# Delta-rule attention and an MLP on one core: another order of ScalarE's and VectorE's work in the opening

## The chip, the core and the metric

The kernel runs on one core of a Trainium2 chip. The core has TensorE (matmul), VectorE, ScalarE, GpSimd, and SyncE, which issues most of the DMAs; the five run at the same time, each takes its own instructions in the order in which they were written, and semaphores hold an instruction until what it needs is there. The metric is the device time of one execution in microseconds (us); lower is better. Times given as medians come from several executions; a profile is of one execution.

## The reference

```python
def _attn_ref(q, k, v, beta):                 # (4, 8, 768, 48): batch, heads, steps, width
    k_n = k / (np.linalg.norm(k, axis=-1, keepdims=True) + 1e-06)
    state = np.zeros((B, H, D, D))
    for t in range(S):
        kt, vt, bt = (k_n[:, :, t], v[:, :, t], beta[:, :, t, None])
        y[:, :, t] = np.einsum('bhd,bhde->bhe', q[:, :, t], state)
        v_old = np.einsum('bhde,bhd->bhe', state, kt)
        state = state + bt[:, :, :, None] * np.einsum('bhd,bhe->bhde', kt, vt - v_old)
    return y

def _moe_ref(x, w_in, w_out):                 # x: y as (3072, 384); d_ff 2048
    h = x @ w_in
    g = h * np.clip(h + 3.0, 0.0, 6.0) / 6.0
    return g @ w_out
```

The output of a recurrent attention (a state matrix for each batch and head, updated by the delta rule) is the input of an MLP with a hard swish.

## The kernel before

**Tiling.** The 768 steps are cut into 24 chunks of 32. A tile has the 4 batches' 32 steps on its 128 partitions. Inside a chunk the recurrence is a triangular system, whose inverse X turns the values less the old state's answer (R) into the new values (Z); between chunks the state is carried on. The MLP takes blocks of two chunks (256 tokens).

**For a chunk t.** `prep` (word p in the list below) scales the keys by their norm (GpSimd, L510), turns keys and queries on TensorE (`pt`, L524), copies them on ScalarE (`KQ`, L532), makes the scores on TensorE (`sc`, L547) and takes them out on VectorE with a mask (`L` and `LB`, L558). `chain` (h) reads the state (`ks`, L806), makes R (L901, L909), applies X (`pz`, L827), copies the result to Z on ScalarE (tile `R`, L927), and updates the state (`su` L938, `state` L956). Its output part (y) makes y (`py` L827; for chunk 0 a copy on ScalarE, L861), turns it (`yt`, L873) and copies it to `xT` on ScalarE (L877), the MLP's input.

**The inverses.** Chunk 0 has its own (`product`). Chunks 1 to 4 are one group: `halves_of` (word i1) waits for the scores of all four, transposes them (L469), eliminates the halves of all problems step by step on VectorE (L730, L735; 28 small instructions in a chain) and transposes back (L473). `join` (x1, x2, ...) then makes one chunk's inverse whole: a transpose (L694), a product on TensorE (`pi`, L684), L698 and L702 on VectorE, a second `pi`, and a copy to `X` on ScalarE (L710). `pz` of that chunk waits for this copy.

**The weights.** `w_in` and `w_out` arrive in a wide format in 16 pieces, 0 to 15 (word w issues a load) and are converted. ScalarE does four steps for a piece (word a, `scales`, L356), VectorE three (word c, `convert`: L378, L383, L389). The last of VectorE's steps needs all four of ScalarE's; and ScalarE's first step of piece i writes the buffer that VectorE's last step of piece i - 2 reads.

**The MLP in the opening.** The first half block (token half a) is made as soon as chunk 0's `xT` is there: word ua issues the products for 128 columns of `w_in` (`ph`, L994; "two more chunks" in the change are two such words), ra their relu on ScalarE (L1001), and ga the "rest", a minimum and product on VectorE (L1004), after which the PSUM buffer is free. There are four such buffers, shared with `pt`, `pi`, `pz`, `py`, `yt`.

**What sets the order.** Everything up to chunk 5 and the first three down and up passes is written in the order of a list of words, `ORDER`: each word runs one step of one of these generators, and `x*3` is three steps. A step's instructions go to the end of their engines' queues. So the list alone decides what stands ahead of what on each engine; an assertion (`needs`) refuses a list in which a step's inputs have not been issued. After the list a plan in the loop over chunks takes over; it is the same in both kernels.

Of the kernel before, what the change touches and what calls it, by code (L numbers as in the profile page):

```python
# [22 lines left out]
k*2 B*3 k*2 n0 k*2 z B s*2 n0*6 k*2 q*2 n1 q n1 q w k p0 z*3 k n1*2 k*2 n1*2 z p0*2 s k p0*3 a k a  # L23
m0 a n2 m1 p0 x0*2 w q x0 n1 x0*3 c*2 n2 a k s p1*2 a s*2 k q s*2 x0 n2 k*2 c x0 n2 x0 w q a*4 q p1
n2 k*2 a x0 m2 p1 c*2 p1 n2*3 b1 q b0 s p1 x0 q w x0 n2 q*2 c*3 x0 n4 k p1 k p2*2 x0*2 a*2 c a*2 q*3
a*2 w v p3*2 q x0 q n4 p2*2 c p2 v c n4*2 a*3 z v n4 c a m3 v c p2 n4*2 q p2 k c b2 h0 c h0 w a*2 h0
p4*2 a*2 m4 p3 q*4 h0 q k w p4*2 c*5 v*2 p3 k p3*3 k*2 p4*2 v*2 p4 m6 k a w a w i1*3 k i1*7 a i1*2 a
i1*2 v i1*2 k b3 k y0 c y0*3 ua*2 ra*2 i1*3 w v ga v a*3 i1*2 ua i1 h1 i1 q w ua ra ua i1 ra*2 ga i1
k ua a*2 ra ga i1 ga ua ra ua ra i1 ga i1*4 ua ga n5 x1*2 k x1 c a ra v a*2 ga x2 k*2 ga*2 ua*2 x1
ra*2 x1*2 ua h1*2 n5 k ga c ra ga*2 h1 c y1*2 ua ra w ga ua ra x2 n5 ga y1*2 ua ra ga h1 v*3 n5*2 k  # L30
y1*2 ua a ra x2 ub*2 a n5 rb*2 h1 x3 ga c*2 v W a h2 y2 gb ub rb gb x2 gb ub*2 n5*2 b4 rb n5 x2*2 h2
gb rb gb m5 a n5*2 y2 ub rb gb v c q*2 v q*5 n5 ub n5 rb gb h2 c h2 q ub y2 h2 y2 rb ub p5 b5 rb
gb*2 a*2 x3 p5 ub y2*2 k p5*2 h2 rb h3 p5 gb h3 ub*2 q rb gb rb gb ub a x3 p6 v c x4 x3 rb gb ub p7
rb gb y3 c*2 v c p7*2 y3 v p7*2 b6 x3 q x3 ub p6 h3 a p6 c p5*2 rb gb k m7 w p6 h3 u p6 k*2 q*3 a*2
y3 a p6 c y3 v y3*2 u n9 v k q a c a c*2 u*2 ru gu w k a*2 c a*2 x4 c*2 ru p7 a gu k u a*2 p7 p6 m8
u*3 a k u*2 k h3 w ru*2 a*2 gu*2 x4 c*2 x4 k c*2 a p8 k a*2 u ru k h3 u*2 h4 ru a b8 gu k gu y4 p8*3
u h4 k*2 c q k*9 q u p8*2 x4 k ru k*2 gu k c n9 q u q*2 p8 k*2 b7 n9*2 i2 u x4 q i2*2 q ub ru gu u
rb gb i2*2 h4*2 u*2 i2 ru i2*6 y4 i2 gu i2*7 u i2 ru gu i2 u*3 ru i2*4 gu ru i2*2 v i2 c gu u*3 a u
ru c i2 u*2 i2 gu i2*3 q i2*5 y4 h4 n9 i2 e*2 n9*2 i2*4 q i2 y4 e n9 u ru i2*3 u i2 ru*2 gu h4 u n9
i2*2 u i2 e i2*6 y4 u k n9*3 u gu i2 y4 n9 i2 p9 q i2*2 gu  # L40
"""


# [1521 lines left out]
```

## Time and profile before

| | us |
|---|---|
| median of 3 runs | 663.66 |
| lowest, highest | 663.46, 663.9 |
| the profiled execution | 662.06 |
| its span in the profile | 660.3 |
| TensorE busy in the span | 632.5 (96%) |
| VectorE busy | 499.2 (76%) |
| ScalarE busy | 282.3 (43%) |
| GpSimd busy | 225.1 (34%) |

The shares are averages over the whole span. The page's second part cuts the span into 40 slices of 16.5 us and gives each engine's busy tenths in each; the changed words act in slices 3 to 5. The granted TensorE clock of the whole execution is 0.997 of full speed. In ten-microsecond windows of the opening, TensorE is busy 6.33 us (30 to 40), 6.16 (40 to 50), 9.42 (50 to 60) and 9.06 (60 to 70); VectorE 8.82, 9.25, 9.28 and 9.41; ScalarE 7.71, 9.38, 7.08 and 7.21. TensorE's matmuls are pipelined and their ends are modelled, so a full TensorE is not TensorE at its peak.

### The profile page before, as it was taken

The numbers are of one execution on the slowest core, as the hardware profiler recorded it, in microseconds if no ns is written. First come the engines' busy times: TensorE is split into PE (matmuls) and PEld (weight loads), VectorE is DVE, ScalarE is ACT, GpSimd is POOL, SyncE is SP. The second block draws the span as 40 slices with busy tenths as digits, with TensorE's granted clock in tenths as the row PEclk, the third lists the DMA queues.
The fourth block names the chain that finished last, engine by engine and source line by source line (L and its number), as shares of the span: only waits on it lengthen the run. The fifth ranks groups of instructions, "written<-read, shape, count | busy, mean of one in ns | idle before, by whom it ended". The sixth has DMA issues, their size and how long they took to land.

```text
span 660.3 us, 26640 instructions
## 1 busy us (share of the span) xinstructions
PE 632.5 (96%) x11640; PEld 569.2 (86%) x11640; DVE 499.2 (76%) x1170; ACT 282.3 (43%) x548; POOL 225.1 (34%) x352
## 2 busy tenths in 40 slices
PE   2768999999999999999999999999999999999997
PEld 2658987776689989999999999999999999999997
DVE  5899877798657988758988848979658998456354
ACT  5887689332243154154154244244244144153250
POOL 6531022003661353553254354164051242331430
PEclk9998999999999999999999999999999999999999
DMA  7888346202040030041030030020020020000000
GB/s 174 204 198 235 77 102 164 51 25 43 9 87 18 3 74 3 3 90 22 3 74 3 2 74 3 2 63 2 3 50 2 3 49 3 23 18 2 26 1 24
DMA packets 88692, 33.28 MB, mean 50 GB/s; under 512 B 80224, under 2 KB 83424, under 8 KB 88576
## 3 DMA queue, kind: packets, MB, share of 16 engines
q1 hardware_dynamic: 88224, 31.29, 20.8%
q8 instruction: 91, 1.49, 0.9%
q10 hardware_dynamic: 352, 0.30, 0.2%
q14 instruction: 25, 0.20, 0.1%
HBM read 26.84 MB, written 4.72 MB: 48 GB/s over the span
## 4 chain that ended last, share of the span: by engine, by line
PE 91%; DVE 3%; DMA 2%; SPq 1%; ACT 1%; issue 1%; DVEq 0%
PE po L1226 28%; PE ph L1066 27%; PE ph L994 9%; PE po L1162 6%; PE ks L806 4%; PE su L938 3%; PE pt L524 3%; PE pz L827 3%; PE py L827 3%; PE sc L547 2%; PE yt L873 1%; DMA spare<-in_moe_w_in_dram 1%; PE pi L684 1%; DMA w_out<-in_moe_w_in_dram 1%; SPq L168 1%
## 5 line engine op out<-in xcount | busy, mean ns | idle before, releaser
L1066 PE MATMUL ph<-xT,w_in 128*128 128x128 f32 (+1 forms) x720 | 156.8, 321 | 0.0
L1030 POOL TENSOR_TENSOR g<-g 128x256 f32<-128x256 f32 (+1 forms) x144 | 88.6, 616 | 104.7 <-ACT g L1080 99.1
L1066 PEld LDWEIGHTS ph<-xT,w_in 128*128 128x128 f32 x720 | 116.8, 191 | 6.7
L1226 PE MATMUL po<-w_out,g 128*128 128x192 f32 x640 | 110.6, 326 | 0.0
L1226 PEld LDWEIGHTS po<-w_out,g 128*128 128x128 f32 x640 | 104.6, 190 | 0.5
L1080 ACT ACTIVATE g<-ph 128x512 f32<-128x512 f32 x72 | 43.1, 598 | 105.1 <-PE ph L1066 105.1
L1226 PE MATMUL po<-spare,g 128*128 128x192 f32 x480 | 86.7, 332 | 0.0
L1226 PEld LDWEIGHTS po<-spare,g 128*128 128x128 f32 x480 | 77.2, 190 | 1.8
L994 PE MATMUL ph<-xT,w_in 128*128 128x128 f32 (+1 forms) x384 | 72.0, 338 | 0.6 <-ACT xT L877 0.6
L1236 POOL TENSOR_TENSOR o<-o,u 128x192 f32<-128x192 f32 x18 | 13.3, 739 | 163.8 <-ACT o L1233 86.6
L994 PEld LDWEIGHTS ph<-xT,w_in 128*128 128x128 f32 x384 | 59.6, 195 | 7.7 <-ACT xT L877 0.8
L1093 DVE TENSOR_TENSOR g<-ph,g 128x256 f32<-128x256 f32 x72 | 30.2, 419 | 46.8 <-PE ph L1066 33.5
L759 DVE TENSOR_TENSOR pr<-A 128x30 f32<-128x30 f32 (+9 forms) x150 | 57.3, 382 | 3.3
L1212 DVE TENSOR_TENSOR g<-g 128x512 f32<-128x512 f32 x80 | 56.1, 722 | 3.5 <-PE po L1226 3.5
L1113 DVE SCALAR_TENSOR_TENSOR g<-o,g 128x512 f32<-128x512 f32 x72 | 52.6, 730 | 7.8 <-ACT o L1110 7.7
L764 DVE TENSOR_TENSOR A<-A,pr 128x30 f32<-128x30 f32 (+9 forms) x150 | 55.1, 367 | 3.3
L1110 ACT ACTIVATE o<-g,halves 128x512 f32<-128x512 f32 x72 | 52.2, 725 | 11.3 <-DVE g L1113 8.4
L1066 PE MATMUL ph<-beta_tok,sums_in 128*128 128x128 f32 x288 | 55.9, 275 | 0.0
L356 ACT ACTIVATE spare<-spare,places 128x768 uint16<-128x768 uint16 (+1 forms) x56 | 52.8, 947 | 3.2 <-DMA kf<-in_k_dram 1.6
L1233 ACT ACTIVATE o<-po 128x192 f32<-128x192 f32 x40 | 13.3, 332 | 82.7 <-PE po L1226 79.2
L510 POOL TENSOR_TENSOR kb<-kf,inv 128x384 f32<-128x384 f32 x24 | 21.7, 907 | 75.5 <-issue 43.1
L1162 PE MATMUL po<-w_out,g 128*128 128x384 f32 x128 | 45.4, 490 | 0.0
(141 smaller groups left out, 1019.1 us busy)
## 6 DMA issues: line engine op xcount, KB each, us to landing
kf<-in_k_dram SPq DMA_DIRECT2D x96, 48.0 KB, 2.6
qb<-in_q_dram SPq DMA_DIRECT2D x96, 48.0 KB, 2.4
vf<-in_v_dram SPq DMA_DIRECT2D x96, 48.0 KB, 2.1
out_dram<-o SPq DMA_DIRECT2D x90, 48.0 KB, 1.6
spare<-in_moe_w_in_dram SPq DMA_DIRECT2D x4, 768.0 KB, 6.6
w_out<-in_moe_w_in_dram SPq DMA_DIRECT2D x4, 768.0 KB, 6.1
w_out<-in_moe_w_out_dram SPq DMA_DIRECT2D x4, 768.0 KB, 5.8
spare<-in_moe_w_out_dram SPq DMA_DIRECT2D x4, 768.0 KB, 5.2
```

The costliest lines, as they stand in the source:

```text
L356: nc.scalar.activation(out=z, in_=z if n else d.bitcast(I16)[:, :, :, 3], func=func, bias=places[:, n : n + 1], scale=scale,)
L759: nc.vector.tensor_tensor(out=pv, in0=A[:, j + 1 :, j].unsqueeze(2).to_broadcast([n, w, j]), in1=A[:, j, 0:j].unsqueeze(1).to_broadcast([n ...
L764: nc.vector.tensor_tensor(out=A[:, j + 1 :, 0:j], in0=A[:, j + 1 :, 0:j], in1=pv, op=ALU.subtract)
L994: nc.tensor.matmul(ph[:, cols], lhsT=w_in[:, s, f * 128 : (f + 1) * 128], rhs=xT[:, s, cols], start=(s == 0), stop=(s == NKT - 1),)
L1030: nc.gpsimd.tensor_tensor(out=out, in0=a, in1=b, op=op)
L1066: nc.tensor.matmul(ph[:, n], lhsT=w, rhs=x, start=start, stop=stop, skip_group_check=True)
L1080: nc.scalar.activation(out=gt, in_=ph[:], func=ACTF.Copy)
L1110: nc.scalar.activation(out=r, in_=g, func=ACTF.Relu, bias=half, scale=1.0 / 6.0)
L1113: nc.vector.scalar_tensor_tensor(out=g, in0=r, scalar=1.0, in1=g, op0=ALU.min, op1=ALU.mult)
L1162: nc.tensor.matmul(pos[c][:], lhsT=gs[blk, f // 2][:, f % 2, c * P : (c + 1) * P], rhs=w_out[:, f, :], start=(f == 0), stop=(f == NFC - 1),)
L1212: nc.vector.tensor_tensor(out=A(f, *out, 4), in0=A(f, *a, 4), in1=A(f, *b, 4), op=op)
L1226: nc.tensor.matmul(ps[n][:], lhsT=A(f - f % 2, *a)[:, f % 2], rhs=b[:, f], start=(f == 0), stop=(f == HF - 1),)
```

## The change

Only the list of words differs; it has 782 words in both kernels, and each word occurs as often. ScalarE's copies of Z of chunk 0 (called R in the kernel's tiles), of the turned keys and queries of chunks 3 and 4, and of y of chunk 0 are issued ahead of conversion steps that stood before them. VectorE's steps of the conversion stand at other places: three of them (L389 of one piece, L378 and L383 of the next) stood ahead of the scores of chunks 3 and 4 and are issued later. Two more words ua (two column groups of the first half block) stand ahead of the first product of the join of chunk 1, and the words ra, ga and c around it move with them. TensorE turns the queries of chunk 3 ahead of `su`. GpSimd's and SyncE's orders stay as they were.

As instructions, from the fourth scale step of piece 3 on: ScalarE before had the four scale steps of piece 4, R, four of piece 5, keys 3, keys 4, queries 3, queries 4, four of piece 6, y, xT. ScalarE now has two of piece 4, R, keys 3, one, queries 3, one, one of piece 5, keys 4, queries 4, two, y, one, four of piece 6, xT. Further on, piece 8's four scale steps stood between the relus and stand now together behind relu 10, ahead of relu 11 and the first copy to X.

The diff (of the list's lines that differ, up to the last word that does):

```diff
-a*2 w v p3*2 q x0 q n4 p2*2 c p2 v c n4*2 a*3 z v n4 c a m3 v c p2 n4*2 q p2 k c b2 h0 c h0 w a*2 h0
-p4*2 a*2 m4 p3 q*4 h0 q k w p4*2 c*5 v*2 p3 k p3*3 k*2 p4*2 v*2 p4 m6 k a w a w i1*3 k i1*7 a i1*2 a
-i1*2 v i1*2 k b3 k y0 c y0*3 ua*2 ra*2 i1*3 w v ga v a*3 i1*2 ua i1 h1 i1 q w ua ra ua i1 ra*2 ga i1
-k ua a*2 ra ga i1 ga ua ra ua ra i1 ga i1*4 ua ga n5 x1*2 k x1 c a ra v a*2 ga x2 k*2 ga*2 ua*2 x1
-ra*2 x1*2 ua h1*2 n5 k ga c ra ga*2 h1 c y1*2 ua ra w ga ua ra x2 n5 ga y1*2 ua ra ga h1 v*3 n5*2 k
+a*2 w v p3*2 q x0 q n4 p2*2 c p2 v c n4*2 a*2 z v n4 c m3 v c p2 n4*2 q p2 k c b2 h0*2 p3 a w p3*2
+h0 a h0 p4*2 p3 a m4 q*4 c p3 q k w p4*2 c p4*2 c v*2 p4 k*3 v*2 a m6 k y0 a y0 a*2 w a w i1*3 k
+i1*7 a i1*2 a i1*2 c v i1*2 k b3 k y0*2 ua*2 ra*2 i1*3 w v ga v a*3 i1*2 ua i1 h1 i1 q w ua ra ua i1
+ra*2 ga i1 k ua a ra ga i1 ga ua ra ua ra i1 ga i1 ua i1*2 ra ga ua ra ga i1 n5 x1*2 ga c*2 k ua x1
+c a c a v a*2 x2 k*2 ga x1 ra x1*2 ua h1*2 n5 k ga c ra ga*2 h1 c y1*2 ua ra w ga ua ra x2 n5 ga
...
```

More of the change, by code (lines that the diff above doesn't have):

```diff
@@ L30 @@
-ra*2 x1*2 ua h1*2 n5 k ga c ra ga*2 h1 c y1*2 ua ra w ga ua ra x2 n5 ga y1*2 ua ra ga h1 v*3 n5*2 k
[L31 to L39, printed above, removed]
@@ L40 @@
-i2*2 u i2 e i2*6 y4 u k n9*3 u gu i2 y4 n9 i2 p9 q i2*2 gu
+a*2 w v p3*2 q x0 q n4 p2*2 c p2 v c n4*2 a*2 z v n4 c m3 v c p2 n4*2 q p2 k c b2 h0*2 p3 a w p3*2
[3 more added lines that the diff above has]
+c a c a v a*2 x2 k*2 ga x1 ra x1*2 ua h1*2 n5 k ga c ra ga*2 h1 c y1*2 ua ra w ga ua ra x2 n5 ga
@@ new lines @@
+y1*2 ua ra ga h1 v*3 n5*2 k y1*2 ua a ra x2 ub*2 a n5 rb*2 h1 x3 ga c*2 v W a h2 y2 gb ub rb gb x2
+gb ub*2 n5*2 b4 rb n5 x2*2 h2 gb rb gb m5 a n5*2 y2 ub rb gb v c q*2 v q*5 n5 ub n5 rb gb h2 c h2 q
+ub y2 h2 y2 rb ub p5 b5 rb gb*2 a*2 x3 p5 ub y2*2 k p5*2 h2 rb h3 p5 gb h3 ub*2 q rb gb rb gb ub a
+x3 p6 v c x4 x3 rb gb ub p7 rb gb y3 c*2 v c p7*2 y3 v p7*2 b6 x3 q x3 ub p6 h3 a p6 c p5*2 rb gb k
+m7 w p6 h3 u p6 k*2 q*3 a*2 y3 a p6 c y3 v y3*2 u n9 v k q a c a c*2 u*2 ru gu w k a*2 c a*2 x4 c*2
@@ L41 @@
+ru p7 a gu k u a*2 p7 p6 m8 u*3 a k u*2 k h3 w ru*2 a*2 gu*2 x4 c*2 x4 k c*2 a p8 k a*2 u ru k h3
+u*2 h4 ru a b8 gu k gu y4 p8*3 u h4 k*2 c q k*9 q u p8*2 x4 k ru k*2 gu k c n9 q u q*2 p8 k*2 b7
+n9*2 i2 u x4 q i2*2 q ub ru gu u rb gb i2*2 h4*2 u*2 i2 ru i2*6 y4 i2 gu i2*7 u i2 ru gu i2 u*3 ru
+i2*4 gu ru i2*2 v i2 c gu u*3 a u ru c i2 u*2 i2 gu i2*3 q i2*5 y4 h4 n9 i2 e*2 n9*2 i2*4 q i2 y4 e
+n9 u ru i2*3 u i2 ru*2 gu h4 u n9 i2*2 u i2 e i2*6 y4 u k n9*3 u gu i2 y4 n9 i2 p9 q i2*2 gu
 """
```

## The prediction

> **What bounds the kernel now.** I read the page first: slices, then the chain that ended last.
>
> ```profile
> span 660.3 us, 26640 instructions
> PE   2768999999999999999999999999999999999997
> ## 4 chain that ended last, share of the span: by engine, by line
> PE 91%; DVE 3%; DMA 2%; SPq 1%; ACT 1%; issue 1%; DVEq 0%
> ```
>
> TensorE is full from the fourth slice on, and the list of its waits has none between 62 and 655 us. So a delay of TensorE at about 65 us reaches the end whole, and only the opening, before about 61 us, has idle time to save. The changed words act from 36 to 70 us. Next the timeline of that stretch, TensorE first:
>
> ```profile
> 36.03 1.50 PE L827 MATMUL pz<-vf,X 32*32 32x48 f32 x64
> 39.29 1.27 PE L938 MATMUL su<-R,sums_in 32*64 32x48 f32 x61 [1.75 <-ACT R L927]
> 41.31 0.44 PE L938 MATMUL su<-R,sums_in 32*64 32x48 f32 x3 [0.75 <-issue]
> 49.92 0.55 PE L873 MATMUL yt<-ident,y 128*128 128x128 f32 x3 [2.41 <-ACT y L861]
> 61.24 0.72 PE L684 MATMUL pi<-X,sums_in 16*32 16x16 f32 x64 [0.94 <-DVE sums_in L694]
> 63.43 0.73 PE L684 MATMUL pi<-X,sums_in 32*32 32x16 f32 x64
> 64.95 0.95 PE L827 MATMUL pz<-R,X 32*32 32x48 f32 x64
> ```
>
> Columns are start, duration, engine, line and tile, and in brackets the wait. See the two waits for ScalarE (R, y), a hold of 0.75 us in the middle of `su` that no engine ended ("issue"), and the wait of the first join product `pi` for VectorE. ScalarE and VectorE in the same stretch:
>
> ```profile
> 38.77 0.47 ACT L927 ACTIVATE R<-pz 128x384 f32<-128x384 f32 x1
> 45.51 3.98 ACT L356 ACTIVATE spare<-spare,places 128x768 uint16<-128x768 int16 x4
> 50.51 0.49 ACT L877 ACTIVATE xT<-yt 128x384 f32<-128x384 f32 x1 [0.64 <-PE yt L873]
> 53.62 2.93 ACT L356 ACTIVATE spare<-spare,places 128x768 uint16<-128x768 int16 x3
> 56.46 0.78 ACT L1001 ACTIVATE g<-ph,halves 128x128 f32<-128x128 f32 x2
> 64.22 0.28 ACT L710 ACTIVATE X<-pi 128x128 f32<-128x128 f32 x1
> ```
> ```profile
> 47.70 1.93 DVE L469 STREAM_TRANSPOSE A<-L 128x1024 f32<-128x1024 f32 x1
> 57.36 0.28 DVE L1004 SCALAR_TENSOR_TENSOR g<-g,ph 128x128 f32<-128x128 f32 x1
> 60.74 0.45 DVE L694 STREAM_TRANSPOSE sums_in<-X 128x256 f32<-128x256 f32 x1
> 62.54 0.44 DVE L702 STREAM_TRANSPOSE sums_in<-sums_in 128x256 f32<-128x256 f32 x1
> ```
>
> VectorE waits only once between 36 and 69 us (0.47 us, for `su`): from 42 to 63 it is the bound. The third relu on ScalarE (56.46) is used by VectorE at 57.36, only 0.5 us after it ends.
>
> **The change, part by part.** No instruction is added or taken away. On GpSimd and SyncE the built order is the same, row by row, so no DMA is issued past another; their waits move with the engines they wait for, and the pieces of weights needed here (the last issued at 44.99, median 7.0 us to land) come before their first use. On ScalarE, VectorE and TensorE the rows change places up to the second join product; each engine has the same rows before its part of the join's last step. So nothing is gained by work, only by waits, and the most that can be gained at that step is small: VectorE's one wait (0.47 us) plus the 0.45 us by which `pi` at 63.43 starts after VectorE's L702 ended (62.98): 0.9 us.
>
> (1) R, turned keys and queries, y ahead of conversions. R now stands behind two scale steps (0.95 each) instead of four; they end at 36.93, the product `pz` at 37.53, so R runs at 37.6 to 38.05 instead of 38.77 to 39.24: 1.2 us earlier. TensorE meanwhile turns the queries of chunk 3 (0.95: half of the 1.91 for two such), and `su` starts at 38.45. What the trace does not show is whether the hold inside `su` goes with it. Queue 8, kind instruction, moves 91 packets in the run, one for about 256 of TensorE's 23,280 instructions, and a packet runs between 38.2 and 39.9; the hold ends at 41.31. I read it as code arriving late. Bounds: the code comes by the time and is not helped by an earlier start (41.31 stays), or the hold vanishes (`su` ends at 40.15). All that precedes the fetch is unchanged, so I take the first and keep the second as a rival. Then `su` ends at 41.8 as before. The keys of chunk 4 are turned by 42.65, its queries (after scores 3, 1.1) by 44.7, and scores 4 run from 45.25 to 46.0. ScalarE has done its earlier work by then and waits: 0.64 for `pz`, 0.7 for the keys, 1.5 for the queries. Before, it waited 0.29 and, at xT, 0.64. After queries 4 (45.2) come two scale steps (47.1), y (47.5, instead of 49.87), then five scale steps (4.8) which now stand ahead of xT: xT runs at 52.3 instead of 50.51. Setting y aside early moves TensorE's wait of 2.41 us to the next step and adds 1.8. What waits for xT: the first up product, 52.8 instead of 51.05.
>
> (2) Three of VectorE's conversion steps later. `state` ends at 42.75, one conversion step (0.95) by 43.7, scores 3 out by 44.55, two steps by 46.05, scores 4 out by 46.85. The transpose L469 starts there, 0.85 us earlier than 47.70. The elimination behind it is as long as before up to the third "rest" of the MLP (57.36 - 47.70 = 9.66), which would fall at 56.5. But that needs the third relu, which stands behind three scale steps and the second up product: 56.46 + 2.1 (1.75 of xT, the rest from slower matmuls) = 58.55, done at 58.9. VectorE waits 2.4 us with the elimination behind it, and TensorE's join behind that.
>
> (3) Two more chunks ahead of the first join. TensorE's two groups (0.77 each) lie beside VectorE's work and cost nothing there; if VectorE were 0.5 us faster they would be late themselves. Their two "rests" now stand before the transpose L473 and need relus 6 and 7, behind a scale step: about 60.8 and 61.1. So L473 runs from 61.35 to 63.2, L694 to 63.6, and the first `pi` starts at 63.65 instead of 61.24. Between it and the second `pi` TensorE has nothing, while VectorE does a rest (0.2), two converting steps L378 (0.5 each), L383 (0.97), L389 (0.97), a rest (0.2), and only then L698 and L702 (0.75): 67.7. The second `pi` starts at 67.75, not 63.43.
>
> (4) A new wait. The conversion of weight piece 6 (L389) ends at about 66.25 in that row. Piece 8's four scale steps reuse its buffer, and on ScalarE all four now stand ahead of relu 11 and of the copy X (L710). Four steps (3.8): 70.1; relu and copy: 70.7. `pz`, which needs X, starts at 70.7 instead of 64.95.
>
> The sum, stage by stage: xT +1.8, first join product +2.4, second +4.3, `pz` **+5.7 us**. Behind `pz` the order is the old one and TensorE was never idle. The profiled execution took 662.06 us (span 660.3 and 1.8 around it); it becomes 667.8. The median of the runs stands 1.6 us above that execution, 663.66, so I forecast 663.66 + 5.7 = **669.4 us**.
>
> **The rivals.**
>
> The code comes earlier. If the hold in `su` vanishes, xT comes at 50.2, the third relu ends at 56.5, L694 at 61.3 and piece 6's L389 at 63.95; scale steps, relu and X end at 68.4, and `pz` is 3.4 us late: **667.1 us**. For it: only one such hold is in the stretch. Against it: it ended 1.5 us after its packet, whose start did not wait for `su`.
>
> TensorE's clock. The profile of before has this row (last but two, the granted clock):
>
> ```profile
> 52.00:54.00 2.00, 2.00 (x12) 2.00 (x11) 1.79 (x8) 1.01 (x3) 0.00 (x0) 0.50 1.08 312
> ```
>
> It follows waits of 2.41 and 0.58 us. The changed kernel has 3.4 us of idle between the two `pi`, and 1.5 more ahead of `pz`. If half clock still holds for 1.6 us of full work behind `pz`, 0.8 us are lost; if it holds one stretch of 3.4 us longer, 2.5: **670.2 to 671.9 us**. [...]
>
> Faster: VectorE's earlier start gets through. The mechanism is L469 at 45.2 (no hold) with relu 3 in time, so that the elimination never stops. It decides only where relu 3 ends before 54.9 and X is not kept behind piece 8. The bound in the part above allows 0.9 us at the second join: **662.8 us**, which is within 0.2% (1.3 us, about what a measurement of this kernel can tell from no change). With the scale steps of piece 8 still ahead of X, even this case ends at +0.7, 664.4. To be faster by more needs a cost of before that I do not see, for example contention.
>
> **How the numbers follow.** Forecast as summed: 0.45. Code earlier: 0.20. Clock on top: 0.26. Within 0.2%: 0.06. Faster: 0.03. So slower 0.91. The range leaves out the last two and a little at the top: from 666.3 (the 3.4 less 0.8 for roundings of the hand sum) to 672.2 us.
>
> **What would show it.** Right: R at about 37.6 and y at about 47.1 in ScalarE's timeline, yet xT later than 50.5; VectorE waiting 1.5 us or more for a relu at 55 to 59; TensorE idle about 3 us between the two `pi` (for L702) and again ahead of `pz` (for X, ScalarE). Wrong: xT before 50, no wait of VectorE for the third relu, piece 8's scale steps starting before 62, or `pz` before 66.

## The result, and the profile after

The changed kernel is slower: 670.49 us median of 6 runs (669.87 to 677.23) against 663.53 us (662.48 to 663.9) for the kernel before on the same chip, a ratio of 1.0133, 95% interval 1.0089 to 1.0177. The ratio is taken over all runs, two of which took 675.16 and 677.23 us; the two medians alone would give 1.0105. The prediction was 669.4 us, 666.3 to 672.2: the direction is right and the median lies in the range, but by the ratio the 663.66 us shown before become 672.5, 0.3 above the range's top. The profiled execution took 670.70 us (span 668.9), 8.6 more than the one before.

The page of the changed kernel: the span, TensorE's slices, and the chain that ended last.

```profile
span 668.9 us, 26639 instructions
PE   2767899999999999999999999999999999999997
## 4 chain that ended last, share of the span: by engine, by line
PE 92%; DMA 2%; ACT 2%; DVE 1%; SPq 1%; issue 1%
```

Before, TensorE's fourth and fifth slices held 8 and 9 tenths; now they hold 7 and 8. TensorE's own timeline there (start, duration, engine, line, tile, shapes, count; in brackets its idle time and what ended it):

```profile
40.59 0.33 PE L938 MATMUL su<-R,sums_in 32*64 32x48 f32 x7 [2.29 <-issue]
48.05 0.90 PE L873 MATMUL yt<-ident,y 128*128 128x128 f32 x3 [0.61 <-ACT y L861]
53.02 4.21 PE L994 MATMUL ph<-xT,w_in 128*128 128x128 f32 x18 [4.07 <-ACT xT L877]
64.93 0.73 PE L684 MATMUL pi<-X,sums_in 16*32 16x16 f32 x64 [0.64 <-DVE g L1004]
68.93 1.05 PE L684 MATMUL pi<-X,sums_in 32*32 32x16 f32 x64 [3.27 <-DVE sums_in L702]
71.74 1.50 PE L827 MATMUL pz<-R,X 32*32 32x48 f32 x64 [0.19 <-ACT X L710]
73.17 2.56 PE L994 MATMUL ph<-xT,w_in 128*128 128x128 f32 x12
77.35 0.89 PE L938 MATMUL su<-R,bkb 32*64 32x48 f32 x64
```

The wait for y, 2.41 us before, has become one of 0.61 us, and there is a new one of 4.07 us for xT. Between the two `pi`, where there was TensorE work and no wait, there are 3.27 us of idle. `pz` of chunk 1 starts at 71.74 instead of 64.95. And two rows are longer than they were: `pz` 1.50 us for 0.95, the twelve `ph` behind it 2.56 for 1.60. The rows of the kernel before for `y`, these `ph` and `su`:

```profile
49.40 0.47 ACT L861 ACTIVATE y<-py 128x384 f32<-128x384 f32 x1
65.83 1.60 PE L994 MATMUL ph<-xT,w_in 128*128 128x128 f32 x12
69.05 0.89 PE L938 MATMUL su<-R,bkb 32*64 32x48 f32 x64
```

In the changed kernel, ScalarE and VectorE show whom TensorE waited for:

```profile
47.50 0.49 ACT L861 ACTIVATE y<-py 128x384 f32<-128x384 f32 x1 [1.15 <-PE py L827]
52.50 0.47 ACT L877 ACTIVATE xT<-yt 128x384 f32<-128x384 f32 x1
67.37 1.00 ACT L356 ACTIVATE spare<-w_out,places 128x768 uint16<-128x768 int16 x1 [2.93 <-DVE w_in L389]
71.42 0.27 ACT L710 ACTIVATE X<-pi 128x128 f32<-128x128 f32 x1
```
```profile
46.85 1.94 DVE L469 STREAM_TRANSPOSE A<-L 128x1024 f32<-128x1024 f32 x1
59.45 0.29 DVE L1004 SCALAR_TENSOR_TENSOR g<-g,ph 128x128 f32<-128x128 f32 x1 [2.42 <-ACT g L1001]
62.26 1.97 DVE L473 STREAM_TRANSPOSE X<-A 128x1024 f32<-128x1024 f32 x1
68.43 0.45 DVE L702 STREAM_TRANSPOSE sums_in<-sums_in 128x256 f32<-128x256 f32 x1
```

y is set aside 1.9 us earlier than before, xT 2.0 us later. VectorE starts the group's transpose L469 0.85 us earlier and then stands 2.42 us at the third rest for relu 3. ScalarE, 2.93 us idle, waits with piece 8's scale steps for piece 6's L389, and X stands behind them. The clock in two-microsecond windows (granted TensorE clock third from the right):

```profile
66.00:68.00 2.00, 0.00 (x0) 0.00 (x0) 1.93 (x4) 0.63 (x1) 0.00 (x0) 1.00 0.38 39
70.00:72.00 2.00, 1.81 (x20) 1.52 (x24) 2.00 (x5) 1.93 (x5) 1.08 (x2) 0.50 0.42 87
72.00:74.00 2.00, 2.00 (x68) 1.88 (x60) 1.15 (x3) 0.69 (x2) 0.00 (x0) 0.50 0.31 60
76.00:78.00 2.00, 2.00 (x121) 1.81 (x110) 0.99 (x3) 0.92 (x3) 0.00 (x0) 1.00 0.03 8
```

Behind the 3.27 us of idle between the two `pi` the granted clock is 0.50 for 6.83 us, from 68.39 to 75.22. Before, it was 1.00 there (all windows from 56 to 70 us).

### The profile page after: what moved, and what is told of

It reads as the page before. It is cut to its first block, busy times and chain, and to the rows that moved or that the text cites. A ratio compares the mean times of both kernels' runs of the same rounds, so it can differ in the third digit from the quotient of the medians.

```text
span 668.9 us, 26639 instructions
## 1 busy us (share of the span) xinstructions
PE 636.7 (95%) x11640; PEld 572.1 (86%) x11640; DVE 498.9 (75%) x1170; ACT 281.4 (42%) x548; POOL 224.8 (34%) x352
## 3 DMA queue, kind: packets, MB, share of 16 engines
q8 instruction: 91, 1.49, 0.9%
## 4 chain that ended last, share of the span: by engine, by line
PE 92%; DMA 2%; ACT 2%; DVE 1%; SPq 1%; issue 1%
PE po L1226 28%; PE ph L1066 27%; PE ph L994 10%; PE po L1162 6%; PE ks L806 4%; PE pt L524 3%; PE pz L827 3%; PE py L827 3%; PE su L938 3%; PE sc L547 3%; ACT spare L356 1%; PE yt L873 1%; DMA w_out<-in_moe_w_in_dram 1%; SPq L168 1%; DMA spare<-in_moe_w_in_dram 1%
## 5 line engine op out<-in xcount | busy, mean ns | idle before, releaser
L1066 PEld LDWEIGHTS ph<-xT,w_in 128*128 128x128 f32 x720 | 116.9, 191 | 6.7
L994 PEld LDWEIGHTS ph<-xT,w_in 128*128 128x128 f32 x384 | 61.6, 203 | 11.7 <-ACT xT L877 4.5
L356 ACT ACTIVATE spare<-spare,places 128x768 uint16<-128x768 uint16 (+1 forms) x56 | 52.3, 942 | 2.3 <-DMA kf<-in_k_dram 1.3
```

The source lines that it names most:

```text
L356: nc.scalar.activation(out=z, in_=z if n else d.bitcast(I16)[:, :, :, 3], func=func, bias=places[:, n : n + 1], scale=scale,)
L994: nc.tensor.matmul(ph[:, cols], lhsT=w_in[:, s, f * 128 : (f + 1) * 128], rhs=xT[:, s, cols], start=(s == 0), stop=(s == NKT - 1),)
L1066: nc.tensor.matmul(ph[:, n], lhsT=w, rhs=x, start=start, stop=stop, skip_group_check=True)
```

## The experiments

The theory going in: the new order costs what the prediction summed, and the half clock adds to it. Ratios are always against the kernel before, run beside it on the same chip. A table comes first; its times are those of one profiled execution, the median and the ratio those of all runs. `sc` is the start of the scores that open the stretch, `su` that of chunk 1's state update, which stands behind the join; "su to end" is the rest of the span.

| kernel | sc | sc to su | su to end | median, ratio (95%) |
|---|---|---|---|---|
| before | 34.92 | 34.1 | 591.3 | |
| changed | 33.75 | 43.6 | 591.5 | 670.49, 1.0133 (1.0089–1.0177) |
| changed, again | 34.9 | 41.2 | 592.4 | 670.79, 1.0131 (1.0102–1.0159) |
| changed, beside e13 | 34.7 | 42.0 | 591.4 | 670.71, 1.0132 (1.0083–1.0181) |
| opening's half alone (e3) | 34.5 | 37.7 | 592.3 | 665.23, 1.0040 (1.0024–1.0056) |
| join's half alone (e4) | 34.3 | 36.5 | 591.6 | 665.22, 1.0030 (1.0011–1.0048) |
| conversions put back (e2) | 34.6 | 41.3 | 591.3 | 669.42, 1.0099 (1.0064–1.0134) |
| clock kept up (e1) | 34.6 | 39.0 | 600.2 | 677.50, 1.0220 (1.0186–1.0254) |
| clock up at the join (e8) | 33.3 | 41.8 | 594.7 | 674.20, 1.0176 (1.0144–1.0208) |
| changed, ten matmuls added (e6) | 34.5 | 42.2 | 597.3 | 676.73, 1.0222 (1.0193–1.0252) |
| before, ten matmuls added (e7) | 34.3 | 35.7 | 601.2 | 670.29, 1.0106 (1.0073–1.0139) |
| e7 and 54 at the start (e9) | 35.5 | 36.6 | 591.2 | 665.29, 1.0039 (1.0015–1.0063) |
| e1 and 54 at the start (e11) | 36.4 | 39.2 | 592.1 | 669.75, 1.0100 (1.0040–1.0161) |
| before, 32 at the start (e12) | 35.2 | 39.5 | 596.5 | 673.47, 1.0150 (1.0098–1.0201) |
| clock up, 256 added (e13) | 34.7 | 41.6 | 591.6 | 671.11, 1.0128 (1.0105–1.0151) |
| the same, more at the join (e15) | 34.1 | 40.4 | 593.3 | 670.96, 1.0127 (1.0071–1.0183) |

The first rows already say where the changed kernel's time is: all of it between `sc` and `su`. The added matmuls of the later rows are work that nothing uses (the first y is turned five times instead of once, or products go to free columns of a PSUM bank).

**One half of the change alone.** The list of words was taken from the changed kernel up to the first up products (e3), or from behind them (e4); the rest is the list before. In e3 the three conversion steps of VectorE catch up inside the elimination; in e4 they have been done before, as in the kernel before.

```diff
 e3, against before: the words from "a*2 z" to "y0*2 ua*2" are those of the changed kernel
+y0*2 ua*2 c*3 ra*2 i1*3 ...          (then as before)
 e4, against before: the words from "a*2 ra ga i1" on are those of the changed kernel
+i1 ua i1*2 ra ga ua ra ga i1 n5 x1*2 ga k ua x1 a c a v a*2 x2 ...
```

> The changed kernel's opening on ScalarE and TensorE (R, keys, queries and y early) with the old order from the first up products on: two up products fewer ahead of the join, conversion steps inside the elimination, piece 8's scale steps between the relus. Theory (about half of the loss comes from xT being later and the third relu with it): pz is about 3.8 us late against before, the time 666.5 to 668. Rival (all of the loss is made at the join): 664.5 or less.

> The old opening, and from the first up products on the changed order: two more up products and two more rests ahead of the join, piece 8's scale steps together ahead of the copy to X; the conversion steps are done before. Theory: X waits for piece 8's scale steps, pz is about 1.8 us late against before, the time 664.5 to 666. Rival (the join's new order makes most of the loss): 668 or more; rival (it costs nothing since TensorE has other work): 663.5.

Both cost. The opening alone is 2.7 us by its ratio (0.0040 of 662.38), less than expected; the join alone 2.0 us, as expected. By the profiles they are late by 3.6 and 2.4 us at `su`, counted from `sc`, 6.0 together, where the whole change is late by 7.1 to 10.1 in six profiles. The ratios say the same: 2.7 and 2.0 us against 8.7. So each half does its own harm, and together they do more than the sum. The join's half alone already has the rows of the half clock:

```profile
65.61 1.50 PE L827 MATMUL pz<-R,X 32*32 32x48 f32 x64 [0.28 <-ACT X L710]
67.05 2.12 PE L994 MATMUL ph<-xT,w_in 128*128 128x128 f32 x12
```

**The conversions between the two `pi`.** Of the four conversion steps of VectorE that stand there in the changed kernel, L378, L383 and L389 of piece 6 go back ahead of L469 and into the elimination; one step, L378 of the next piece, stays.

```diff
-... y0 a y0 a*2 w a w i1*3 k         ... x1*2 ga c*2 k ua x1 c a c a v
+... y0 a y0 a*2 c*3 w a w i1*3 k     ... x1*2 ga k ua x1 a c a v
```

> The changed kernel with VectorE's three conversion steps (L389 of piece 5, L378 and L383 of piece 6) ahead of the elimination again, and L389 of piece 6 inside it; ScalarE, TensorE, GpSimd and SyncE as in the changed kernel. Theory (the steps between the two join products cost their own time, and the elimination waits for the third relu anyway): the first join product stays at 64.5 to 65.5, the second comes 2.5 to 3 us earlier, at about 66.2, pz 3 us or more earlier, and the time is 665.5 to 667.5. Rival (the delay is made in the opening, by xT and the hold in su): 669 us or more.

The expectation missed at the end. The gap between the two `pi` closes as expected (0.95 us of wait instead of 3.27), and `pz` comes 34.5 us behind `sc`, in the changed kernel's profiles 35.6 to 38.3. But the rows are those of the half clock all the same, and here `py` has them too (1.50 us; in the changed kernel 0.88):

```profile
69.14 1.50 PE L827 MATMUL pz<-R,X 32*32 32x48 f32 x64 [0.41 <-ACT X L710]
70.58 2.93 PE L994 MATMUL ph<-xT,w_in 128*128 128x128 f32 x12
73.44 1.50 PE L827 MATMUL py<-R,LB 32*32 32x48 f32 x64
```

From `pz` to `su` it takes 6.8 us; in the kernel before 4.1, in the changed kernel 5.2 to 5.9. So a part of the gain is given back before `su`. By the ratios (1.0099 against 1.0131 to 1.0133) about 2 us are left, with intervals that overlap.

**Is it the clock?** Unused matmuls keep TensorE busy in its two idle stretches: four more turns of the first y, and four products of 384 columns between the two `pi`. e8 has only the latter.

```diff
-            for s in range(NKT):
-                nc.tensor.transpose(pt[:, s, :], y[:, s * 128 : (s + 1) * 128], ident[:])
+            for _ in range(5 if t == 0 else 1):
+                for s in range(NKT):
+                    nc.tensor.transpose(pt[:, s, :], y[:, s * 128 : (s + 1) * 128], ident[:])
...
+            if name == "pi1" and t == 1:
+                for _ in range(4):
+                    nc.tensor.matmul(bank[:, 128:512], lhsT=ident[:], rhs=w_in[:, 0, 0:384], ...)
```

> The changed kernel with TensorE kept busy in its two gaps: y of chunk 0 is turned five times over, and four matmuls of 384 columns with unused results follow the first product of the join. Theory (the half clock costs about 2.5 us on top of the waits): the granted clock stays at 1.0 behind the first join, the first 18 up matmuls take under 3.5 us instead of 4.21, pz under 1.1 us instead of 1.50, the two up products behind it 1.6 instead of 2.56, and the kernel takes 666.5 to 668.5 us, 2 to 3.5 us less than the changed kernel's 670.5. Rival (the waits alone set the time and the half clock lies beside them): the clock is full, and the time stays at 669.5 or more.

> The changed kernel with the four matmuls of 384 columns between the two join products, and nothing else added: 16 more instructions of TensorE. Theory (the half clock behind the join costs 2.5 us): the granted clock is not halved at 68 us, pz of chunk 1 takes 0.9 us and not 1.5, the first 18 up matmuls still take 4.2, and the work up to py of chunk 1 ends 2 us or more earlier, counted from the scores of chunk 2; the time is 667 to 668.5 unless holds for code come instead. Rival (the half clock costs nothing): py ends as late as in the changed kernel.

In e1 the granted clock is 1.00 in every window from 46 to 78 us, `pz` takes 0.88 us and `su` comes 2.2 to 5.1 us sooner than in the changed kernel's profiles (39.0 behind `sc` against 41.2 to 44.2). Yet the kernel is slower, 677.5 us, which neither theory expected. The loss is behind `su`, where nothing was changed. Its timeline there has holds that no engine ended, the rows with `<-issue`:

```profile
77.12 0.30 PE L685 MATMUL pi<-X,sums_in 16*32 16x16 f32 x12 [0.88 <-issue]
89.82 0.60 PE L1002 MATMUL ph<-xT,w_in 128*128 128x128 f32 x4 [1.62 <-issue]
102.93 0.27 PE L547 MATMUL sc<-KQ 64*32 64x64 f32 x2 [1.18 <-issue]
108.62 0.33 PE L547 MATMUL sc<-KQ 64*32 64x64 f32 x11 [2.03 <-issue]
```

Counted in TensorE's records (weight loads, matmuls and semaphore instructions, by their start), these stand behind 3009, 3777, 4545 and 4801 of them; the hold in `su` of the kernel before stands behind 1473. All are 193 plus a multiple of 256. In the kernel before, queue 8, kind instruction, moves 1.49 MB in 91 packets of 16.4 KB, one for each 256 of TensorE's instructions. e8 has the full clock only from 56 us on, through the join (`pz` 0.88 us long), and three long holds that no engine ended, 1.7 us in a `yt`, 1.6 in chunk 0's `su` and 0.8 in an `sc`: 674.2 us. So the new theory: TensorE's code comes in packets of 256 instructions, and a packet that is late holds it where the packet begins. 40 added instructions (e1) move every later cut by 40. And TensorE is slower behind a long hold: behind the last of e1's four, four `po` took 2.76 us (109.26), in the changed kernel 1.46 (106.34), where the granted clock is 1.00 from 76 us to the end.

**Do the cuts matter, and how much?** Ten tiny matmuls behind the first yt, where TensorE is idle anyway, in both kernels (40 instructions: each is two weight loads and two matmuls).

```diff
+            for _ in range(10 if t == 0 else 0):
+                nc.tensor.matmul(bank[0:32, 384:400], lhsT=ident[0:32, 0:32],
+                                 rhs=ident[0:32, 0:16], ...)
```

> The changed kernel itself, unchanged, with more runs. Two of its six runs took 675 and 677 us, the others 670. Theory (TensorE's code arrives too late in some runs, between 75 and 110 us): runs fall into two groups again, near 670 and near 676, and if the profile is of a long run it has holds that no engine ended in that stretch, 5 us in all; in a short run none. Rival (the half clock lasts longer in the long runs): the granted clock of the long runs is lower by 0.01 or more than that of the short ones.

> The changed kernel with ten small matmuls (32 by 32 by 16, results unused) behind the first turn of y, in a gap in which TensorE waits 4 us anyway: 40 more of TensorE's instructions, so that its code is cut 40 instructions earlier from there on. Theory (a packet of 256 instructions that comes late holds TensorE wherever the cut falls): holds appear at counts that are 193 more than a multiple of 256, at other places of the program than before, and the time moves by 2 us or more against the changed kernel's 670.5, most likely up, to 673 to 677. Rival (the cuts make no difference): 669.5 to 671.5.

> The kernel before with the same ten small matmuls at the same place. They may make xT up to 0.8 us later, which the elimination on VectorE hides. Theory (the cuts of TensorE's code matter, also without the change): the time moves by 1.5 us or more, up more likely, 664 to 668 where the kernel before has 662.4 in the same runs. Rival (they don't): within 1 us of the kernel before.

The ten cost the changed kernel 6 us (676.73 against 670.79) and the kernel before 7.4 (670.29 against 662.92), more than was expected of the latter. Its profile, of the longest of its four executions (672.83), has lost 1.5 us against the kernel before at `su` and loses 10 us behind it; its four longest holds there:

```profile
73.28 0.30 PE L684 MATMUL pi<-X,sums_in 16*32 16x16 f32 x12 [0.72 <-issue]
86.15 0.60 PE L1000 MATMUL ph<-xT,w_in 128*128 128x128 f32 x3 [1.73 <-issue]
100.76 0.24 PE L547 MATMUL sc<-KQ 64*32 64x64 f32 x1 [1.27 <-issue]
106.15 0.33 PE L547 MATMUL sc<-KQ 64*32 64x64 f32 x11 [1.73 <-issue]
```

These are the instructions that e1 was held at, in a kernel with another order ahead of them: they stand behind 3009, 3777, 4545 and 4801 records again. Behind two of them TensorE is slow: six `ph` at 87.40 took 1.49 us (0.83 at 71.17), and four `po` at 106.79 took 2.45 (1.46 at 101.46).

The next three add matmuls of the same kind at the very start, where TensorE waits for its first keys: 54 (216 instructions), which together with 40 make 256, so that behind the stretch every cut falls where it did; and 32 (128) in the kernel before, with no other edit.

```diff
+    spun = psM.tile([128, 512], FP32, name="spun", tag="pm0")
+    for _ in range(54):          # e12: 32
+        nc.tensor.matmul(spun[0:32, 0:16], lhsT=ident[0:32, 0:32],
+                         rhs=ident[0:32, 0:16], start=True, stop=True)
```

> The kernel before with the ten small unused matmuls behind the first yt (which alone took 7.4 us more) and 54 of the same kind at the very start, where TensorE has nothing to do: 40 + 216 = 256 of TensorE's instructions, so that behind the first yt every packet of its code begins at the same instruction as in the kernel before. Theory of the code (the ten cost their 7.4 us because they moved where packets begin, so that packets come late): the time goes back to the kernel before's, 662 to 665 us, and the holds that no engine ended, at 73, 86, 101 and 106 us, are gone. Rival (the ten matmuls cost by what they do: their time, their PSUM bank, the clock): it stays at 669 to 673 us.

> The same kernel as the first experiment, taken once more without the matmuls at the start, beside the three others: both theories expect 675 to 678 us again.

> The changed kernel with the unused matmuls that keep TensorE's clock up through the join (677.5 us), and 54 tiny ones at the very start: 256 instructions together, so that behind the join every packet of code begins where it does in the changed kernel. Theory (clock and order take the changed kernel's time, the packets took the gain of the full clock back): the holds behind 75 us are gone, and the time is that of the changed kernel less what the full clock brought at py (4.7 us): 665.5 to 668 us. Rival (the unused matmuls themselves cost what the clock brings): 670 us or more.

> The kernel before with 32 tiny matmuls at the very start alone, where TensorE has nothing to do: 128 of its instructions, so that every packet of code begins half a packet earlier in the program. Nothing else is moved. Theory of the code: the holds that no engine ended come at other instructions than before, and the time moves by 1.5 us or more, either way (slower is likelier: the kernel before has hardly any such hold behind 62 us). Rival (code comes in time whatever its cuts): the time stays within 1 us of the kernel before's.

In e9 the cost falls from 7.4 us to 2.7 (665.29 against 662.55; 0.3 above what was expected), and its profile has no such hold at all. e10, e1 run once more, took 673.48, under the 675 to 678 expected. e11 comes down from e1's 677.5 to 669.75, and su to the end from 600.2 to 592.1 us; that lies between the two expectations, and its profile has a new hold of 2.73 us in `py` at 47.7, on a cut that the 54 brought there, and starts the stretch 1.8 us later than e1. e12 is the plainest: nothing but 32 matmuls on an idle engine, and 10.9 us more than the kernel before (673.47 against 662.55; by the ratio 9.9). The matmuls themselves are not what is paid for: e9 has 54 of them there and costs 2.7.

```profile
39.13 0.37 PE L833 MATMUL pz<-vf,X 32*32 32x48 f32 x3 [1.35 <-issue]
53.40 0.55 PE L833 MATMUL py<-R,LB 32*32 32x48 f32 x17 [5.92 <-issue]
88.78 0.69 PE L944 MATMUL su<-R,bkb 32*64 32x48 f32 x42 [0.93 <-issue]
107.14 0.78 PE L553 MATMUL sc<-KQ 64*32 64x64 f32 x55 [1.85 <-issue]
```

The hold of 5.92 us stands behind record 1985, and TensorE went on at 53.40. The trace of the kernel before has a late transfer of queue 8 at that place (50.68 to 51.58; TensorE entered the packet ahead of it, record 1729, at 46.30), but there that packet lasted until 55.22, since TensorE was waiting 2.41 us for y, and nothing shows.

So the cuts are settled as a cause, with sizes up to 10.9 us (e12), the slower matmuls behind a long hold included. They do not explain the changed kernel: it adds no instruction, its cuts behind the join are those of the kernel before, and its time from `su` to the end is the old one.

**The clock again, with the cuts left alone.** The fillers of e1 made up to exactly 256 instructions with tiny matmuls (e13: 16 behind y, two products of 384 columns and 40 tiny ones between the two `pi`; e15: 22, four and 32), and the changed kernel beside them (e14).

```diff
+            for _ in range(2):                    # e15: 4
+                nc.tensor.matmul(bank[:, 128:512], lhsT=ident[:], rhs=w_in[:, 0, 0:384], ...)
+            spin(bank, 40)                        # e15: 32; behind the first yt 16, e15: 22
```

> The changed kernel with unused matmuls in TensorE's two idle stretches (the first y turned five times and 16 tiny matmuls behind it; two matmuls of 384 columns and 40 tiny ones between the two pi), so that its clock stays up, and exactly 256 of its instructions, so that every packet of code begins where it does in the changed kernel, ahead of the stretch and behind it. If half clock is what the prediction's sum lacked: py at 71 to 72 us (the changed kernel 75.67), no hold behind 75 us, and a time of 665 to 668 us against 669.5 to 671.5 for the changed kernel beside it. Rival (the packets or the unused matmuls take it back, or the clock's cost is hidden): 669 us or more.

> The changed kernel unchanged, beside the run with the clock kept up: 669.5 to 671.5 us.

> As the run before with 256 added instructions, but four matmuls of 384 columns and 32 tiny ones between the two pi (instead of two and 40) and 22 tiny ones behind the first y (instead of 16). There the clock was full from 52 to 69 us and fell to half at 69, so pz, three up products and py ran slow all the same. Here the work between the two pi is that with which the first experiment kept it full. If half clock behind the join is what is left to explain: granted clock 1.0 from 52 us to the end of py, pz 0.9 and py 0.9 us long, su of chunk 1 about 39.0 to 39.5 us behind the scores that open the stretch (changed kernel 41.2 to 43.6), and a time of 666.5 to 669 us. Rival (it comes back later, or is covered): 669.5 us or more.

Neither gets faster at the end: 671.11 and 670.96 against 670.71 for e14. In e13 the clock is full only from 52 to 68 us. First `pi`, second `pi` and `pz` come 1.3 us sooner than in e14 (62.91, 66.91 and 69.72), the scores that open the stretch at the same time; so that much is the half clock ahead of the join (0.50 from 52 to 56 us in e14). Then it falls, and the gain is gone by `su` (0.3 left):

```profile
68.00:70.00 2.00, 0.77 (x21) 0.58 (x23) 2.00 (x6) 1.90 (x5) 1.06 (x2) 0.64 0.32 57
70.00:72.00 2.00, 2.00 (x67) 1.88 (x56) 1.14 (x3) 0.59 (x2) 0.00 (x0) 0.50 0.41 74
```

In e15 it stays at 1.00 from 56 us to past `py`, which comes 38.7 us behind `sc` instead of 40.3. But a dense TensorE is held there too: `su`, in one piece in the changed kernel, breaks, and so does a `ph` behind it. (The first row below is a hold inside the added matmuls.)

```profile
51.30 0.30 PE L215 MATMUL yt<-ident 32*32 32x16 f32 x12 [3.02 <-issue]
75.65 0.74 PE L959 MATMUL su<-R,bkb 32*64 32x48 f32 x47 [0.76 <-issue]
79.48 0.71 PE L1015 MATMUL ph<-xT,w_in 128*128 128x128 f32 x5 [0.30 <-issue]
```

So the half clock stands on the path as far as `su`. But no form that takes it away brings more at the end than e11's 1 to 2 us (by the median 669.75, by the ratio 1.0100): in e13 it came back later, in e1, e8 and e15 holds came in its place. That part of the expectations was wrong, and what a full clock would be worth without them was not measured.

**Long executions.**

> The changed kernel unchanged, a profile of one more execution. 4 of its 16 times so far are 673.9 to 677.2 us, the rest 668.8 to 671.4. If this one is long: theory of the code, holds that no engine ended, behind 77 us, at counts 256 instructions apart, that add up to the excess, with su of chunk 1 where it was; rival, the excess lies before su. If it is not long: as the profiles before, no hold behind 77 us, 591 to 592.5 us from su to the end.

> As the run before it: the changed kernel once more, for a profile of a long execution.

> As the two runs before it: the changed kernel once more, for a profile of a long execution.

They took 671.60, 671.57 and 670.79 us, and none was long: `sc` to `su` 43.6, 44.2 and 42.7, `su` to end 591.9, 591.6 and 591.6. 4 of 19 executions of the changed kernel took 673.9 to 677.2 us. None of them has a profile, so the theory on them (code that comes late behind `su`) was never put to the test. Their mean granted clock, 0.959 to 0.985, does not set them apart from the other 15, 0.969 to 0.995. Why they are long stays open.

## Why the prediction was right in its steps and wrong in its sum

Six profiles of the changed kernel hold the steps' times. Three of them against the forecast (us from the span's start):

| step | forecast | first profile | again (e5) | beside e13 (e14) |
|---|---|---|---|---|
| y | 47.1 | 47.50 | 46.32 | 46.74 |
| xT | 52.3 | 52.50 | 51.33 | 51.74 |
| VectorE's wait for relu 3 | 2.4 | 2.42 | 2.27 | 2.27 |
| first `pi` | 63.65 | 64.93 | 63.73 | 64.22 |
| second `pi` | 67.75 | 68.93 | 67.72 | 68.21 |
| `pz` | 70.7 | 71.74 | 70.53 | 71.03 |
| `su` (4.1 behind `pz`) | 74.8 | 77.35 | 76.12 | 76.66 |
| `pz`, counted from `sc` | 35.8 | 38.0 | 35.6 | 36.3 |

Steps (1) to (4) are right wait by wait: y early and xT late, VectorE stopped by relu 3, TensorE empty between the two `pi`, X behind piece 8. In e5 the three products (both `pi` and `pz`) come within 0.2 us of the forecast, partly by luck, since two errors offset each other: xT 1.0 us early, and half clock under the first up products (4.21 us for 18, before 3.55). e5's profile:

```profile
67.72 1.05 PE L684 MATMUL pi<-X,sums_in 32*32 32x16 f32 x64 [3.27 <-DVE sums_in L702]
70.53 1.50 PE L827 MATMUL pz<-R,X 32*32 32x48 f32 x64 [0.18 <-ACT X L710]
71.97 2.55 PE L994 MATMUL ph<-xT,w_in 128*128 128x128 f32 x12
```

Step (1), the hold in `su`: taken to end at 41.31 whatever precedes it. In the five profiles that have it in `su` it ended at 40.44 to 41.57, and there the rival of earlier code did not happen. But it is not one number: it spreads by 1.1 us, and in e5 it came one packet earlier, ahead of chunk 0's `pz`, and `su` ran unbroken. `pz` of chunk 1 spreads from 70.53 to 72.28 over the six, where the forecast has 70.7; counted from `sc` it comes at 35.6 to 38.3, on average 37.3, where the forecast has 35.8.

**The step that failed is the sum's last, which puts the clock at nothing**: "Behind `pz` the order is the old one and TensorE was never idle". The order is the old one; the rate is not. The term for the clock was kept out of the sum as a rival with a chance of 0.26, at 0.8 or 2.5 us. That rival happened in every profile of the changed kernel: from `pz` to `su` 5.2 to 5.9 us instead of 4.1, so 1.1 to 1.8 more, between the rival's two values. No run shows the 1.6 us of half clock that the rival has behind `pz`, and its 3.4 us is the length of the half clock in the kernel before (51.80 to 55.22); in the changed kernel the clock was at 0.50 for 6.83 us, 3.5 of them from `pz`'s start on (71.74 to 75.22). The prediction had the evidence: it computed an idle time of 3.4 us between the two `pi`, and showed the row in which waits of 2.41 and 0.58 us were followed by half clock. With this term, 5.7 + 1.5 = 7.2, the forecast would have been 670.9 us; the median was 670.5. The same term is too small ahead of the join, where step (2) has it only as "the rest from slower matmuls", 0.35 us: from xT to the first `pi` the forecast allows 11.35 us, the six profiles took 11.8 to 12.8, and e13 and e1, with the clock full there, 10.4. So some 1.1 us more of half clock lie there. The two, 1.5 and 1.1, are most of what the sum lacks: counted from `sc`, `su` is late by 7.1 to 10.1 us, 8.8 on average, where the sum has 5.7. The last 0.5 us stay open; the kernel before has only one profile to count from.

The range failed at its top: it had no case for executions longer by 3 to 7 us, and two such among six carry the ratio past 672.2. The other four alone average 670.25 us, which against the 663.43 of the kernel before's six makes a ratio of 1.0103, 670.5 us.

The ceiling (nothing to gain but 0.9 us) is not contradicted by any run: no kernel here beats the one before. The rival of the other sign, VectorE's earlier start getting through, needed relu 3 before 54.9; it ended at 59.4.

## What to carry to other kernels

In an opening in which several engines are full, an early result is worth what its consumer's queue lets through: follow it to the consumer, and look at what the work put behind it now makes late (here y 1.9 us earlier, xT 2.0 us later). Where a new order leaves TensorE idle as here (3.27 us, and behind it 6.83 us at half clock), put the half clock into the sum and not beside it. And on a kernel whose TensorE executes many tiny matmuls, as this one does, compare variants whose counts of TensorE instructions ahead of the dense part are equal or 256 apart; here 40 added instructions cost the kernel before 7.4 us (e7) and 128 cost it 10.9 (e12).

## What the runs showed of the hardware

The holds whose place was counted lie 256 of TensorE's records or a multiple apart (behind 1473, 1985, 3009, 3777, 4545 and 4801), and queue 8, kind instruction, has 91 packets of 16.4 KB in the kernel before, one for each 256 of TensorE's 23,280 weight loads and matmuls (92 in e7, which has 40 more). That these packets are TensorE's code is the author's reading of the two. The queue's packets beside TensorE's records give the rest, with an entry at each 256th record from 193 on. In the kernel before between 62 and 100 us, the next packet's transfer began 0.6 to 1.2 us after TensorE entered one and took 0.9 to 1.3 us; between 25 and 58 us, with a DMA share of 0.80 to 0.97 against 0.30 to 0.46 later, it began 1.7 to 4.4 us after the entry. Where TensorE was held at a cut, it went on 1.5 us after the transfer's end (before, 39.81 to 41.31) and 1.6 us (changed kernel, 39.01 to 40.59). A packet runs for 3.4 to 4.3 us between 62 and 100 us, which is about what this adds up to (3.0 to 4.1, an estimate from the figures above): adding 40 and 128 instructions cost 7.4 and 10.9 us.

The clock also fell where no single idle stretch was long. In e13 none between 53 and 68.5 us was longer than 0.99 us, and the clock's mean is 0.64 from 68 to 70 us and 0.50 from 70 to 74, so it was at half from about 68.6 on. TensorE's busy time beside the clock, in stretches of 3.41 us (the half clock of the kernel before lasted that long): in the changed kernel TensorE is busy for 0.68 us from 64.98 to 68.39, with the idle between the two `pi`, at a clock of 1.00; for 2.69 us in the next stretch and all of the third, both at 0.50; from 75.22 on the clock is 1.00. In the kernel before it is busy for 1.30 us from 48.39 to 51.80, at 1.00; all of the next stretch, at 0.50; and from 55.22 on the clock is 1.00. In e13 the 3.41 us ahead of 68.6 have TensorE busy for 2.4 us, added up from its timeline; in e1 those up to 68.5 have 2.5 us, and there the clock stayed at 1.00. What decides between these cases was not shown.

One reading of the kernel before has to be taken with care: its trace has no record of the clock before 44.98 us, and the profile then prints 1.00. Its `pz` at 36.03 took 1.50 us, as chunk 1's does in the changed kernel at a clock of 0.50 (71.74); in e1 the same product took 0.88 (35.40), as chunk 1's does there at 1.00 (69.52). So the opening before was probably in part at half clock as well, and its 0.997 for the whole execution too high; that is an estimate from these lengths.
